# Linear attention before a mixture of experts: q·k in four 64x64 tiles ahead of the state's outputs, the state updated in the turn that made it, k and the rows turned at the turn's end

## The chip, the cores and the metric

The kernel runs on one core of a Trainium2 chip. The metric is the device time of one execution in microseconds (us); lower is better. The kernel before takes 355.63 us (median of three runs, 355.38 to 355.9).

## What is computed

```python
# attention: q, k, v, f_logit are (B=4, H=8, S=768, D=48), float32
f = 1 / (1 + exp(-f_logit))
for t in range(S):
    state = f[:, :, t, :, None] * state + einsum('bhd,bhe->bhde', k[:, :, t], v[:, :, t])
    y[:, :, t] = einsum('bhd,bhde->bhe', q[:, :, t], state)
x = y.transpose(0, 2, 1, 3).reshape(3072, 384)
# mixture of 8 experts: every token goes to the one with the largest logit
e = argmax(x @ w_gate); gate = softmax(x @ w_gate)[e]
out = gate * sigmoid(x @ w_output_gate)[e] * (relu(x @ w1[e]) @ w2[e])
```

## The kernel before

**Two stages.** The attention stage walks over 24 turns t = 0 to 23: four batches b, each of six chunks c = t % 6 of C = 128 steps. The eight heads lie in NP = 4 pairs, a pair on the two halves of the 128 partitions. The expert stage follows: matmuls of line L804 (tokens by w1) and L824 (by w2) with their splits, from about 121 us to the end.

**A chunk.** The decays inside a chunk become running products: `prep(t)` makes f (L209, ScalarE), the products p (`scan_p`, L214, VectorE), their inverses (`scan_i`, L219 and L221, VectorE), and multiplies k and q by them (L225 and L228, GpSimd). What is left is matmuls on TensorE (PE):

- `qk(t)`, L250: k·q of the chunk, per pair two matmuls with 64 rows (a head's half of the partitions) and 128 columns of weights, into two PSUM banks `a_ps`, one for each head of a pair. `mask(t)` copies one bank with ScalarE (L255) and masks it on GpSimd (L256), and masks the other on VectorE (L259); the result is `at`.
- `kn_tr(t)`, L267: k turned, copied by `evac_kn` (L275, ScalarE). No batch's last chunk (c = 5) needs it.
- `out_state(t)`, L310: the state ahead of the chunk by q, in 64x64 tiles, and `out_at(t)`, L318: `at` by v. Both add into y, which lies in two PSUM banks, `two` and the upper half of `one`. The first chunk (c = 0) has no state.
- `state(t)`, L283: turned k by v into the lower half of bank `one`. `state_upd(t)` adds it to the old state and decays it (L297 and L298, VectorE).
- `evac_y(t)`, L332: ScalarE copies y, half a bank at a time, into `xt`; `x_tr(t)`, L338: TensorE turns `xt` into token rows and makes the gate's logits; `evac_x(t)`, L345 and L346: ScalarE copies logits into `lgp` and the rows into `xn`.

**Routing.** After every four turns (two near the end) `route` puts eight small steps into a list: seven VectorE operations (L393 on `lgp`, L396, L397, L398, L400, L401, L391) and one that lets `slots` be made. `fill` takes steps off this list, one or a few at a place. `slots` issues its matmuls at the end of a turn (L424 and L426) into columns of bank `two`, and VectorE reads them (L432, L434). After that, GpSimd sends token rows away with indirect DMAs (L355). The first steps stand in turns 6, 10, 14, 18 and 20, the rank matmuls at the end of turns 7, 11, 15, 19 and 21.

**What sets the order.** Every engine runs its instructions in the order in which the program issues them, and the order of a turn is written out by hand in the loop over t. For each engine of a turn it is, before: TensorE `qk(t)`, `kn_tr(t)`, `x_tr(t-2)`, `out_state(t-1)`, `out_at(t-1)`, `state(t-1)`, ranks; VectorE `state_upd(t-2)`, `scan_p(t+2)`, half of `mask(t)`, `scan_i(t+2)`, with fills between. Loads of later batches are issued on SP's queue at the end of turns (`load`, L183 for v and L190 for q, k and f).

Of the kernel before, what the change touches and what calls it, by code (L numbers as in the profile page):

```python
# [21 lines left out]
C = 128  # L22
NCH = S // C
NP = H // 2
# [8 lines left out]
T_END = 20  # L33
# [24 lines left out]
def warm_up(nc, k, ps, n):  # L58
    for _ in range(n):
        nc.tensor.matmul(ps, k.warm[:, 0:128], k.warm, start=True, stop=True)  # L60
# [72 lines left out]
def attention(ctx, tc, nc, k, kpool, rt, q01, k01, f01, q23, k23, f23, v, wg, xs_dram, r, ex):  # L133
# [14 lines left out]
    q_t = [pl.tile([128, NP, S], F32, name=f"q_t{i}") for i, pl in enumerate((pe, pers))]  # L148
    k_t = [pl.tile([128, NP, S], F32, name=f"k_t{i}") for i, pl in enumerate((pe, pers))]
# [13 lines left out]
    one = psB.tile([128, 512], F32, name="one_ps")  # L163
# [71 lines left out]
    at, aps, kn, xt, xps, yps = {}, {}, {}, {}, {}, {}  # L235
    scomp = {}

    def hot(t):
        return 0 <= t < len(order)

    def qk(t):

        b, c = order[t]
        sl = slice(c * C, (c + 1) * C)
        at[t] = wk.tile([128, 2, NP, C], F32, name="at")
        aps[t] = [psA.tile([128, NP, C], F32, name="a_ps", bufs=2) for par in range(2)]
        for g in range(NP):
            for par in range(2):
                r = slice(64 * par, 64 * par + 64)
                nc.tensor.matmul(aps[t][par][:, g, :], k_t[b % 2][r, g, sl], q_t[b % 2][r, g, sl],  # L250
                                 start=(g == 0), stop=(g == NP - 1))

    def mask(t, par):
        if t == 0 or par:
            nc.scalar.activation(out=at[t][:, par], in_=aps[t][par], func=AF.Copy)  # L255
            nc.gpsimd.affine_select(out=at[t][:, par], in_=at[t][:, par], pattern=[[0, NP], [1, C]],  # L256
                                    compare_op=ALU.is_ge, fill=0.0, base=0, channel_multiplier=-1)
            return
        nc.vector.tensor_tensor(out=at[t][:, par], in0=aps[t][par], in1=k.mask, op=ALU.mult)  # L259

    def kn_tr(t):
        b, c = order[t]
        if c == NCH - 1:
            return
        kps = psA.tile([128, NP, 128], F32, name="kn_ps")
        for g in range(NP):
            nc.tensor.transpose(out=kps[:, g, :], in_=k_t[b % 2][:, g, c * C:(c + 1) * C], identity=k.ident)  # L267
        kn[t] = kps

    def evac_kn(t):  # L270
        if t not in kn:
            return
        kps = kn[t]
        kn[t] = wk.tile([128, NP * 128], F32, name="kn")
        nc.scalar.copy(out=kn[t], in_=kps.rearrange("p g t -> p (g t)"))  # L275

    def state(t):
        b, c = order[t]
        if c == NCH - 1:
            return  # L280
        for h in range(H):
            g, r0 = h // 2, 64 * (h % 2)
            nc.tensor.matmul(s_ps[r0:r0 + 64, g, 0:D], kn[t][:, 64 * h:64 * h + 64],  # L283
                             v_t[b][:, c, 64 * h:64 * h + D],
                             start=(h < 2), stop=(h >= 6), skip_group_check=True)

    def state_upd(t):
        b, c = order[t]
        if c == NCH - 1:
            return  # L290
        end = r.pend[:, t * NP:t * NP + NP].unsqueeze(2).broadcast_to([128, NP, D])
        scomp[t] = states[t % 2]
        new, kv = scomp[t][:, :, 0:D], s_ps[:, :, 0:D]
        if c == 0:
            nc.vector.tensor_tensor(out=new, in0=kv, in1=end, op=ALU.mult)
        else:
            nc.vector.tensor_tensor(out=stmp, in0=kv, in1=scomp[t - 1][:, :, 0:D], op=ALU.add)  # L297
            nc.vector.tensor_tensor(out=new, in0=stmp, in1=end, op=ALU.mult)  # L298
# [23 lines left out]
    def out_y(t):  # L322

        y_at(t)
        out_state(t)
        out_at(t)

    def evac_y(t, halves=(1, 0)):
        if t not in xt:
            xt[t] = wk.tile([128, NP, C], F32, name="xt")  # L330
        for i in halves:
            nc.scalar.copy(out=xt[t][:, i::2, :], in_=yps[t][i])  # L332

    def x_tr(t):

        xps[t] = psB.tile([128, 512], F32, name="x_ps")[:, 0:NP * XW].rearrange("p (g e) -> p g e", e=XW)
        for g in range(NP):
            nc.tensor.matmul(xps[t][:, g, :], xt[t][:, g, :], turn[:, g, :], start=(g == 0), stop=(g == NP - 1))  # L338

    def evac_x(t):  # L340
        if t % 4 == 0:
            xn[t // 4] = xnp.tile([128, 4, RW], F32, name="xn")
            nc.gpsimd.iota(out=xn[t // 4][:, :, DM], pattern=[[C, 4]], base=t * C, channel_multiplier=1,
                           allow_small_or_imprecise_dtypes=True)
        nc.scalar.copy(out=lgp[:, t % 8, :].rearrange("p (g e) -> p g e", e=2 * E), in_=xps[t][:, :, 2 * D:XW])  # L345
        nc.scalar.copy(out=xn[t // 4][:, t % 4, 0:DM].rearrange("p (g e) -> p g e", e=2 * D),  # L346
                       in_=xps[t][:, :, 0:2 * D])
# [18 lines left out]
    def fill(n=1):  # L366
        for _ in range(min(n, len(dq))):
            dq.pop(0)()

    def drain():  # L370
        while dq:
            dq.pop(0)()

    def run_pq(n=None):
        n = len(pq) if n is None else n
        todo, pq[:] = pq[:n], pq[n:]
        for f in todo:
            f()
# [88 lines left out]
    last = len(order) - 1  # L467
# [11 lines left out]
    def pre(t, *names):  # L479
        if hot(t):  # L480
            for nm in names:
                if nm not in done[t]:
                    done[t].add(nm)
                    pre_of[t][nm]()
# [20 lines left out]
    ends, t0 = {}, 0  # L505
# [3 lines left out]
    for t in range(last + 1):  # L509
        ready = len(pq)  # L510
        more = 1 if t < T_END else 0

        fill(more)
        if hot(t - 2):
            evac_y(t - 2, (1,))
        if t not in (0, 2):
            pre(t + 2, "f")
        if hot(t - 2):
            evac_y(t - 2, (0,))
            state_upd(t - 2)  # L520
        if t == 2:
            pre(4, "f")
        pre(t + 1, "mul_k")
        if t + 1 == last:
            done_sb.close()
            ex.open_early()
        fill(more)
        if t > 1:
            pre(t + 2, "scan_p")
        qk(t)  # L530
        mask(t, 1)
        mask(t, 0)
        if t == 0:
            pre(2, "s", "f")
        pre(t + 2, "scan_p", "scan_i")
        if t == 0:
            pre(2, "mul_k")
        fill(more)
        kn_tr(t)
        if t == 0:  # L540
            warm_up(nc, k, one, 4)
        if hot(t - 2):
            x_tr(t - 2)
        evac_kn(t)
        pre(t + 2, "mul_q", "ends")
        if hot(t - 2):
            evac_x(t - 2)
        if t == last:
            ex.split(1, 0, 1, nc.gpsimd)
            route(*ends[t - 2])  # L550
            drain()
        fill(more)
        if T_END <= t < last:
            fill(8)
        pre(t + 3, "s")
        if t == last:
            done_ps.close()
            ex.open_early_psum()
        if hot(t - 1):
            out_y(t - 1)  # L560
        if hot(t - 1):
            state(t - 1)
        if t == last:
            hand_over()
            break
        run_pq(ready)
        if t >= T_END:
            pre(t + 2, "mul_k")
        if t >= T_SCAT:
            scatter(1 if t < T_END else 2)  # L570

        b, c = divmod(t - 3, NCH)
        if t >= 3 and b + 2 < B and c in (0, 2, 4):
            load(b + 2, [("fkq", c, c + 2)])
            if c == 4:
                load(b + 2, [("v", i, i + 2) for i in range(0, NCH, 2)])
        fill(2 if more else 10)
        fill(2 * more)
        if t - 2 in ends:
            route(*ends[t - 2])  # L580
        if t >= T_END:
            scatter(2)
            if len(ex.apart) == T_TOP:
                ex.tokens_in(0, 0, EARLY // TS)
                ex.load_rest(0)
        if t + 1 == last:
            drain()
            assert ex.xq
            ex.split(1, 0, 0, nc.gpsimd)
# [592 lines left out]
```

## Time and profile before

| what | value |
|---|---|
| median of three runs | 355.63 us (355.38 to 355.9) |
| profiled execution | 355.4 us, span of its profile 353.5 us |
| attention, turns 3 to 22 | 22.31 to 112.94 us of the span |
| last turn and hand-over | 112.94 to 121.45 us |
| expert stage | 121.45 us to the end |
| TensorE busy, share of the span | 339.4 us, 96% |
| VectorE, ScalarE, GpSimd busy | 252.1, 202.6 and 213.6 us |
[...]

The span is what the profile shows from the first instruction to the last; 1.9 us of the profiled time lie around it. A busy share over the whole span is an average of two stages; the stage in which something changes has to be looked at by itself. A TensorE record is one pass of a matmul: a float32 matmul of this stage leaves two (16 of L250 in a turn for eight matmuls).

### The profile page before, as it was taken

What the parts mean: (1) busy time and instruction counts of PE and PEld (TensorE: products, weight loads), DVE (VectorE), ACT (ScalarE), POOL (GpSimd) and SP (SyncE); (2) the same over time, 40 slices, a digit from 0 to 9 for tenths busy, and PEclk for the clock granted to TensorE, in tenths of its full rate; (3) what the DMA queues carried; (4) which work ended last, traced back from release to release, by engine and by line L of the source; (5) the groups of instructions that cost most, each with busy time, mean ns of one, the idle gap of its engine ahead of it and who ended that gap; (6) DMA issues with size and microseconds to landing.
All of it is one profiled execution on the core that took longest, in us unless ns stands there. A gap on an engine that the chain in (4) does not pass through costs nothing.

```text
span 353.5 us, 8664 instructions
## 1 busy us (share of the span) xinstructions
PE 339.4 (96%) x3037; PEld 317.5 (90%) x3037; DVE 252.1 (71%) x514; ACT 202.6 (57%) x508; POOL 213.6 (60%) x252
## 2 busy tenths in 40 slices
PE   8889999999999899998999999999999999999992
PEld 2678988898899799997999999999999999999991
DVE  6998989898998676568866766666776766665700
ACT  3576776776775571544853672673673673675510
POOL 8586789899998861000476375276276276187521
PEclk9999999999999999999999999999999999999998
DMA  7999999999408935989659368459468367420101
GB/s 252 350 359 357 346 281 283 307 279 281 158 32 273 270 119 138 190 269 184 194 171 189 115 189 182 136 173 205 111 198 190 116 193 189 135 81 28 60 26 43
DMA packets 75205, 67.64 MB, mean 191 GB/s; under 512 B 30813, under 2 KB 69481, under 8 KB 75152
## 3 DMA queue, kind: packets, MB, share of 16 engines
q1 hardware_dynamic: 70576, 57.34, 59.0%
q0 software_dynamic: 4576, 9.66, 8.1%
q8 instruction: 26, 0.43, 0.5%
q14 instruction: 27, 0.22, 0.2%
HBM read 54.04 MB, written 13.46 MB: 191 GB/s over the span
## 4 chain that ended last, share of the span: by engine, by line
PE 77%; DVE 8%; issue 4%; ACT 3%; DMA 3%; SPq 2%; POOL 1%; POOLq 0%; DVEq 0%; ACTq 0%
PE h_ps L804 27%; PE y_ps L824 20%; PE x_ps L338 6%; PE a_ps L250 5%; PE y_ps L838 5%; PE two_ps L318 3%; PE two_ps L310 3%; PE one_ps L318 3%; PE kn_ps L267 3%; PE one_ps L283 2%; DVE p L214 1%; DVE i L221 1%; SPq L709 1%; DMA xm<-xs_dram 1%; DMA f_t<-in_f 1%
## 5 line engine op out<-in xcount | busy, mean ns | idle before, releaser
L857 POOL DMA_INDIRECT out<-yr,dst x83 | 90.8, 1094 | 59.7 <-ACT yr L856 35.5
L804 PE MATMUL h_ps<-xh,w1h 128*128 128x400 f32 (+6 forms) x192 | 65.3, 340 | 1.1 <-DVE hl L809 1.1
L804 PE MATMUL h_ps<-xh,w1l 128*128 128x400 f32 (+6 forms) x192 | 65.2, 340 | 0.0
L804 PE MATMUL h_ps<-xl,w1h 128*128 128x400 f32 (+6 forms) x192 | 65.2, 340 | 0.0
L809 DVE SCALAR_TENSOR_TENSOR hl<-h_ps,hh 128x256 fp32r<-128x256 f32 (+6 forms) x72 | 39.1, 544 | 32.2 <-ACT hh L808 31.8
L808 ACT ACTIVATE hh<-h_ps 128x256 fp32r<-128x256 f32 (+6 forms) x72 | 34.8, 483 | 42.2 <-PE h_ps L804 40.7
L824 PE MATMUL y_ps<-hh,w2h 128*128 128x256 f32 (+4 forms) x168 | 56.0, 333 | 0.0
L824 PE MATMUL y_ps<-hl,w2h 128*128 128x256 f32 (+4 forms) x168 | 55.9, 333 | 0.0
L824 PE MATMUL y_ps<-hh,w2l 128*128 128x256 f32 (+4 forms) x168 | 55.9, 333 | 0.0
L668 DVE TENSOR_TENSOR w1l<-w1r,w1h 128x768 fp32r<-128x768 f32 x29 | 27.8, 958 | 15.5 <-ACT w1h L667 15.3
L804 PEld LDWEIGHTS h_ps<-xh,w1h 128*128 128x128 f32 x192 | 36.1, 188 | 2.1 <-DVE hl L809 1.5
L804 PEld LDWEIGHTS h_ps<-xl,w1h 128*128 128x128 f32 x192 | 36.1, 188 | 0.6
L804 PEld LDWEIGHTS h_ps<-xh,w1l 128*128 128x128 f32 x192 | 36.1, 188 | 0.6
L228 POOL TENSOR_TENSOR q_t<-q_t,p 128x512 f32<-128x512 f32 x24 | 30.6, 1273 | 4.6 <-DVE p L214 4.5
L824 PEld LDWEIGHTS y_ps<-hh,w2l 128*128 128x128 f32 x168 | 31.7, 188 | 0.6
L824 PEld LDWEIGHTS y_ps<-hl,w2h 128*128 128x128 f32 x168 | 31.6, 188 | 0.7
L824 PEld LDWEIGHTS y_ps<-hh,w2h 128*128 128x128 f32 x168 | 31.7, 188 | 0.6
L214 DVE TENSOR_TENSOR_SCAN p<-f_ps,start_p 128x511 f32<-128x511 f32 x22 | 28.0, 1274 | 3.7 <-ACT start_p L202 2.0
L668 DVE TENSOR_TENSOR w2l<-w2r,w2h 128x768 fp32r<-128x768 f32 x31 | 29.6, 955 | 1.3 <-ACT w2h L667 0.6
L771 ACT CAST xh<-xr 128x400 fp32r<-128x400 f32 (+6 forms) x24 | 12.2, 517 | 32.0 <-DVE xr L765 32.0
L250 PE MATMUL a_ps<-q_t,k_t 64*128 64x128 f32 x384 | 28.3, 285 | 2.1 <-DVE k_t L225 1.2
L355 POOL DMA_INDIRECT xs_dram<-xn,slot x24 | 24.7, 1029 | 7.8 <-issue 3.8
(165 smaller groups left out, 746.4 us busy)
## 6 DMA issues: line engine op xcount, KB each, us to landing
w1r<-in_w SPq DMA_DIRECT2D x32, 384.0 KB, 5.0
w2r<-in_w SPq DMA_DIRECT2D x32, 384.0 KB, 3.0
v_t<-in_v SPq DMA_DIRECT2D x12, 512.0 KB, 9.1
xs_dram<-empty SPq DMA_DIRECT2D x8, 401.0 KB, 10.8
f_t<-in_f SPq DMA_DIRECT2D x6, 512.0 KB, 9.6
q_t<-in_q SPq DMA_DIRECT2D x6, 512.0 KB
k_t<-in_k SPq DMA_DIRECT2D x6, 512.0 KB, 9.6
f_t<-in_f SPq DMA_DIRECT2D x12, 192.0 KB, 6.7
```

Of the source, the lines that this page charges most:

```text
L214: nc.vector.tensor_tensor_scan(out=flat(d["p"])[:, 1:n], data0=flat(d["f"])[:, 0:n - 1], data1=sp[:, 1:n], initial=sp[:, 0:1], op0=ALU.mul ...
L228: nc.gpsimd.tensor_tensor(out=q_t[i][:, :, sl], in0=q_t[i][:, :, sl], in1=d["p"], op=ALU.mult)
L250: nc.tensor.matmul(aps[t][par][:, g, :], k_t[b % 2][r, g, sl], q_t[b % 2][r, g, sl], start=(g == 0), stop=(g == NP - 1))
L318: nc.tensor.matmul(yps[t][g % 2][r0:r0 + 64, g // 2, :], v_t[b][:, c, 64 * h:64 * h + 64], at[t][:, h % 2, g, :], start=((first or c == 0) ...
L338: nc.tensor.matmul(xps[t][:, g, :], xt[t][:, g, :], turn[:, g, :], start=(g == 0), stop=(g == NP - 1))
L355: i = nc.gpsimd.indirect_dma_start(out=xs_dram, out_offset=bass.IndirectOffsetOnAxis(ap=r.slot[:, t:t + 1], axis=0), in_=xn[t // 4][:, t % ...
L668: (eng or self.nc.vector).tensor_tensor(out=to(lo), in0=of(t), in1=to(hi.bitcast(F32)), op=ALU.subtract)
L804: nc.tensor.matmul(ps[:, 0:n], a[:, c, cs], b, start=(i == 0), stop=(i == 3 * KC - 1))
L808: nc.scalar.activation(out=hi, in_=ps[:, 0:n], func=AF.Relu)
L809: nc.vector.scalar_tensor_tensor(out=lo, in0=ps[:, 0:n], scalar=0.0, in1=hi.bitcast(F32), op0=ALU.max, op1=ALU.subtract)
L824: self.nc.tensor.matmul(self.ys[d][:, c0:c0 + n], a, b, start=(f == 0 and i == 0 and part == 0), stop=(f == KF - 1 and i == 2), skip_group ...
L857: self.other_rows(self.nc.gpsimd.indirect_dma_start(out=self.out.rearrange("n (q w) -> (n q) w", q=NQ), out_offset=bass.IndirectOffsetOnAx ...
```

## The change

`qk` makes each product with 64 instead of 128 columns of weights: 16 matmuls in four 64x64 tiles (two row halves by two column halves) instead of eight in two 64x128 tiles. In the turn's order, `out_state`, `out_at` and `state` of t-1 move up to stand directly behind `qk(t)`, and `kn_tr(t)` and `x_tr(t-2)` come after them. `evac_y(t-1)` and `state_upd(t-1)` are issued in the same turn, where they stood in the next. The logits and rows (`evac_x`) are copied at the turn's end, after `prep`'s small steps. VectorE masks ahead of `scan_p`.

```diff
         for g in range(NP):
-            for par in range(2):
-                r = slice(64 * par, 64 * par + 64)
-                nc.tensor.matmul(aps[t][par][:, g, :], k_t[b % 2][r, g, sl], q_t[b % 2][r, g, sl],
-                                 start=(g == 0), stop=(g == NP - 1))
+            for half in range(2):
+                s0, to = c * C + 64 * half, slice(64 * half, 64 * half + 64)
+                for par in range(2):
+                    r = slice(64 * par, 64 * par + 64)
+                    nc.tensor.matmul(aps[t][par][to, g, :], k_t[b % 2][r, g, s0:s0 + 64], q_t[b % 2][r, g, sl],
+                                     start=(g == 0), stop=(g == NP - 1), skip_group_check=True)
...
         fill(more)
-        if hot(t - 2):
-            evac_y(t - 2, (1,))
-        if t not in (0, 2):
+        if t > 0:
             pre(t + 2, "f")
-        if hot(t - 2):
-            evac_y(t - 2, (0,))
-            state_upd(t - 2)
...
-        if t > 1:
-            pre(t + 2, "scan_p")
         qk(t)
+        mask(t, 0)
         mask(t, 1)
-        mask(t, 0)
...
-        pre(t + 2, "scan_p", "scan_i")
-        fill(more)
-        kn_tr(t)
-        if hot(t - 2):
-            x_tr(t - 2)
-        evac_kn(t)
-        pre(t + 2, "mul_q", "ends")
-        if hot(t - 2):
-            evac_x(t - 2)
+        pre(t + 2, "scan_p")
...
         if hot(t - 1):
             out_y(t - 1)
-        if hot(t - 1):
             state(t - 1)
+            if t < last:
+                evac_y(t - 1, (0,))
+                state_upd(t - 1)
+                evac_y(t - 1, (1,))
+        pre(t + 2, "scan_i")
+        fill(more)
+        if t < last:
+            kn_tr(t)
+            if hot(t - 2):
+                x_tr(t - 2)
+            evac_kn(t)
+        pre(t + 2, "mul_q", "ends")
+        pre(t + 3, "s")
+        if hot(t - 2) and t < last:
+            evac_x(t - 2)
+        fill(more)
```

How an ordinary turn stands on TensorE, before (turn 14, c = 2; names as above, with the columns of one matmul's output and how many in a row):

```order
L250 MATMUL a_ps<-q_t_98,k_t_100 128x128 x8
L267 MATMUL kn_ps<-ident,k_t_100 128x128 x4
L338 MATMUL x_ps<-turn,xt 128x112 x4
L310 MATMUL two_ps<-q_t_98,state_106 64x128 x2
L310 MATMUL one_ps<-q_t_98,state_106 64x128 x2
L310 MATMUL two_ps<-q_t_98,state_106 64x128 x2
L310 MATMUL one_ps<-q_t_98,state_106 64x128 x2
L318 MATMUL two_ps<-at,v_t 64x128 x2
L318 MATMUL one_ps<-at,v_t 64x128 x2
L318 MATMUL two_ps<-at,v_t 64x128 x2
L318 MATMUL one_ps<-at,v_t 64x128 x2
L283 MATMUL one_ps<-v_t,kn 64x48 x8
```

And the same turn after the change, where lines are two higher:

```order
L252 MATMUL a_ps<-q_t_98,k_t_100 64x128 x16
L312 MATMUL two_ps<-q_t_98,state_106 64x128 x2
L312 MATMUL one_ps<-q_t_98,state_106 64x128 x2
L312 MATMUL two_ps<-q_t_98,state_106 64x128 x2
L312 MATMUL one_ps<-q_t_98,state_106 64x128 x2
L320 MATMUL two_ps<-at,v_t 64x128 x2
L320 MATMUL one_ps<-at,v_t 64x128 x2
L320 MATMUL two_ps<-at,v_t 64x128 x2
L320 MATMUL one_ps<-at,v_t 64x128 x2
L285 MATMUL one_ps<-v_t,kn 64x48 x8
L269 MATMUL kn_ps<-ident,k_t_100 128x128 x4
L340 MATMUL x_ps<-turn,xt 128x112 x4
```

The products stand in twice as many matmuls, `out_state` (L312) follows them, and the turned k (L269) and rows (L340) have moved from the second and third place to the end.

VectorE of turn 10, in which the steps of a route begin, before; the row of L297 is the state's update of t-2, L259 the mask:

```order
L393 TENSOR_REDUCE xn<-lgp 128x4x16
L297 TENSOR_TENSOR misc<-one_ps,state_107 128x192
L298 TENSOR_TENSOR state_106<-misc,pend 128x4x48
L396 TENSOR_REDUCE misc<-xn 128x4
L214 SCALAR_TENSOR_TENSOR p<-f_ps,start_p_183 128x511
L259 TENSOR_TENSOR at<-a_ps,mask 128x512
L219 RECIPROCAL start_i_187<-p 128x4
L221 SCALAR_TENSOR_TENSOR i<-f_ps,start_i_187 128x512
L397 TENSOR_TENSOR misc<-xn,misc 128x32
L398 SCALAR_TENSOR_TENSOR misc<-misc,first 128x32
L400 TENSOR_REDUCE first<-misc 128x4
L401 TENSOR_TENSOR ohb<-misc,first 128x32
```

And after, from the first route step of that turn on (L395):

```order
L395 TENSOR_REDUCE xn<-lgp 128x4x16
L398 TENSOR_REDUCE misc<-xn 128x4
L261 TENSOR_TENSOR at<-a_ps,mask 128x512
L214 SCALAR_TENSOR_TENSOR p<-f_ps,start_p_183 128x511
L299 TENSOR_TENSOR misc<-one_ps,state_106 128x192
L300 TENSOR_TENSOR state_107<-misc,pend 128x4x48
L219 RECIPROCAL start_i_187<-p 128x4
L221 SCALAR_TENSOR_TENSOR i<-f_ps,start_i_187 128x512
L399 TENSOR_TENSOR misc<-xn,misc 128x32
L400 SCALAR_TENSOR_TENSOR misc<-misc,first 128x32
L402 TENSOR_REDUCE first<-misc 128x4
L403 TENSOR_TENSOR ohb<-misc,first 128x32
```

The first two route steps have come together ahead of the mask, the mask is ahead of L214, and the state's update (L299 and L300) has moved behind both, to the `state` of the same turn.

## Rows read from the trace of the kernel before

**Rows 1.** The page's head: the span, and busy time of each engine with its share and instructions.

```profile
span 353.5 us, 8664 instructions
...
PE 339.4 (96%) x3037; PEld 317.5 (90%) x3037; DVE 252.1 (71%) x514; ACT 202.6 (57%) x508; POOL 213.6 (60%) x252
```

**Rows 2.** Busy time by stretches: turns 3 to 22, and the expert stage. Columns: stretch, its length, busy time (and records) of PE, weight loads, DVE, ACT and POOL, granted clock, DMA share, GB/s.

```profile
22.31:112.94 90.63, 89.81 (x1440) 80.32 (x1436) 81.87 (x167) 63.98 (x193) 78.46 (x81) 1.00 0.91 266
121.45:353.40 231.95, 223.96 (x1313) 219.06 (x1309) 145.93 (x298) 122.49 (x269) 110.79 (x114) 0.99 0.55 149
```

**Rows 3.** The same view of six single turns: 3, 13 (c = 1), 14 (ordinary), 15 (ordinary, with ranks), 17 (c = 5) and 18 (c = 0).

```profile
22.31:27.49 5.18, 4.90 (x81) 4.20 (x77) 4.84 (x7) 3.35 (x11) 3.84 (x6) 1.00 1.08 358
67.81:71.84 4.03, 4.03 (x62) 3.75 (x60) 3.09 (x5) 3.34 (x10) 3.83 (x5) 1.00 1.09 292
71.84:76.47 4.63, 4.63 (x80) 4.18 (x76) 4.56 (x10) 3.34 (x10) 4.43 (x5) 1.00 1.10 280
76.47:81.32 4.85, 4.85 (x86) 4.37 (x82) 4.32 (x9) 3.27 (x11) 4.66 (x6) 1.00 1.11 275
85.95:90.44 4.49, 4.31 (x77) 3.79 (x73) 3.90 (x7) 2.76 (x9) 4.29 (x5) 1.00 1.01 338
90.44:94.62 4.18, 4.18 (x65) 3.61 (x61) 3.93 (x8) 3.24 (x10) 3.98 (x5) 1.00 0.31 112
```

**Rows 4.** TensorE in order of time, the ordinary turn 14. Columns: start, length (us), line, output and inputs, tile and shape, records merged.

```profile
71.84 1.16 PE L250 MATMUL a_ps<-q_t,k_t 64*128 64x128 f32 x16
72.93 0.66 PE L267 MATMUL kn_ps<-ident,k_t 128*128 128x128 f32 x4
73.43 1.04 PE L338 MATMUL x_ps<-turn,xt 128*128 128x112 f32 x8
74.40 0.33 PE L310 MATMUL two_ps<-q_t,state 64*64 64x128 f32 x2
74.41 0.33 PE L310 MATMUL one_ps<-q_t,state 64*64 64x128 f32 x2
...
74.56 0.28 PE L310 MATMUL two_ps<-q_t,state 64*64 64x128 f32 x2
...
74.78 0.28 PE L310 MATMUL two_ps<-q_t,state 64*64 64x128 f32 x2
...
75.00 0.44 PE L318 MATMUL two_ps<-at,v_t 128*64 128x128 f32 x4
...
75.92 0.62 PE L283 MATMUL one_ps<-v_t,kn 128*64 128x48 f32 x16
```

**Rows 5.** VectorE in order of time, turns 10 and 11 and the read of the ranks in turn 12; the same columns, some instructions left out.

```profile
53.98 0.56 DVE L393 TENSOR_REDUCE xn<-lgp 128x64 f32<-128x256 f32 x1
...
55.61 0.20 DVE L396 TENSOR_REDUCE misc<-xn 128x4 f32<-128x32 f32 x1
55.71 1.27 DVE L214 TENSOR_TENSOR_SCAN p<-f_ps,start_p 128x511 f32<-128x511 f32 x1
...
57.69 1.22 DVE L221 TENSOR_TENSOR_SCAN i<-f_ps,start_i 128x512 f32<-128x512 f32 x1
58.83 0.18 DVE L397 TENSOR_TENSOR misc<-xn,misc 128x32 f32<-128x32 f32 x1
...
59.86 0.36 DVE L297 TENSOR_TENSOR misc<-one_ps,state 128x192 f32<-128x192 f32 x1
...
60.53 1.27 DVE L214 TENSOR_TENSOR_SCAN p<-f_ps,start_p 128x511 f32<-128x511 f32 x1
61.72 0.67 DVE L259 TENSOR_TENSOR at<-a_ps,mask 128x512 f32<-128x512 f32 x1
...
62.50 1.22 DVE L221 TENSOR_TENSOR_SCAN i<-f_ps,start_i 128x512 f32<-128x512 f32 x1
...
63.80 0.19 DVE L432 TENSOR_TENSOR rk<-two_ps,ohb 128x32 f32<-128x32 f32 x1
```

**Rows 6.** ScalarE in order of time, the second half of turn 10.

```profile
56.08 0.58 ACT L275 COPY kn<-kn_ps 128x512 f32<-128x512 f32 x1
57.02 0.20 ACT L231 COPY pend<-p 128x4 f32<-128x4 f32 x1 [0.35 <-DVE p L214]
57.12 0.20 ACT L345 COPY lgp<-x_ps 128x64 f32<-128x64 f32 x1
57.22 0.48 ACT L346 COPY xn<-x_ps 128x384 f32<-128x384 f32 x1
57.59 0.22 ACT L202 ACTIVATE start_p<-f_t 128x4 f32<-128x4 f32 x1
57.90 0.19 ACT L204 COPY p<-start_p 128x1 f32<-128x1 f32 x1
```

**Rows 7.** Waits between 22 and 113 us: who waited for whom, us in total, times, longest. These are two of them.

```profile
ACT xt L332 <- PE one_ps L283: 13.3, 16, 1.1
...
PEld x_ps L338 <- ACT xt L332: 1.6, 4, 0.5
```

**Rows 8.** SP's queue around 61 us, first the order of the loads, then the time from issue to landing of the one v load issued between 60.8 and 61.5 us, and of all three issued between 58 and 72 us.

```profile
60.59 1.78 SPq L183 DMA_DIRECT2D v_t<-in_v  x3
...
DMA to landing us min/median/max: 8.4/8.4/8.4
DMA to landing us min/median/max: 8.4/9.1/9.8
```

More of the change, by code (lines that the diff above doesn't have):

```diff
@@ L513, in attention @@
         fill(more)
-        if hot(t - 2):
-            evac_y(t - 2, (1,))
-        if t not in (0, 2):
+        if t > 0:
             pre(t + 2, "f")
-        if hot(t - 2):
-            evac_y(t - 2, (0,))
-            state_upd(t - 2)
-        if t == 2:
-            pre(4, "f")
         pre(t + 1, "mul_k")
@@ L527, in attention @@
         fill(more)
-        if t > 1:
-            pre(t + 2, "scan_p")
         qk(t)
+        mask(t, 0)
         mask(t, 1)
-        mask(t, 0)
         if t == 0:
             pre(2, "s", "f")
-        pre(t + 2, "scan_p", "scan_i")
-        if t == 0:
-            pre(2, "mul_k")
-        fill(more)
-        kn_tr(t)
-        if t == 0:
-            warm_up(nc, k, one, 4)
-        if hot(t - 2):
+        pre(t + 2, "scan_p")
+        if t == last:
             x_tr(t - 2)
-        evac_kn(t)
-        pre(t + 2, "mul_q", "ends")
-        if hot(t - 2):
             evac_x(t - 2)
-        if t == last:
             ex.split(1, 0, 1, nc.gpsimd)
@@ L551, in attention @@
             drain()
[L552 to L556, printed above, removed]
             done_ps.close()
@@ L560, in attention @@
             out_y(t - 1)
-        if hot(t - 1):
             state(t - 1)
+            if t < last:
[3 more added lines that the diff above has]
+        pre(t + 2, "scan_i")
+        if t == 0:
+            pre(2, "mul_k")
+        fill(more)
+        if t < last:
+            kn_tr(t)
+            if t == 0:
+                warm_up(nc, k, one, 4)
+            if hot(t - 2):
[6 more added lines that the diff above has]
+        fill(more)
+        if T_END <= t < last:
+            fill(8)
         if t == last:
```

## The prediction

> **What bounds the kernel now.** I read the page's head first: TensorE is busy for 96% of the span [rows 1]. As this is a mean over two stages, the view by stretches comes next. From turn 3 to turn 22 TensorE is busy for 89.81 of 90.63 us at full clock; VectorE has 81.87 there, GpSimd 78.46, ScalarE 63.98 [rows 2]. So TensorE sets the pace of attention, but VectorE has only 9 us less work. The expert stage, which the change doesn't touch, is bound by TensorE too (223.96 of 231.95 us [rows 2]): what attention gains or loses ahead of 121.45 us is passed on to the end.
>
> The stretches of single turns show what a turn costs: 4.63 us for an ordinary one, 4.03 without `out_state` (c = 1), 4.18 without `state` (c = 0), 4.49 without the turned k (c = 5), .22 more where ranks are computed (4.85), and 5.18 in turn 3 [rows 3]. In all but turns 3 and 17 TensorE is busy for the whole turn, so a turn is the sum of its blocks. The timeline of turn 14 gives these: qk 1.09 (71.84 to 72.93), turned k .50, rows .97, `out_state` .60, `out_at` .92, `state` .55 (75.92 to 76.47, the end of the stretch) [rows 3, 4].
>
> **What TensorE saves.** In `out_state`, four 64x64 tiles run side by side and each such group takes .11 us (74.56 to 74.78 are two), but the first group takes .16 and the last .22 (74.78 to 75.00) [rows 4]. The first and the last stand where the form of the tiles changes, and I read the .05 and .11 over as the price of a change of form. qk has eight pairs of records now: eight times .11 is .88, and the remaining .21 of its 1.09 is such a price at both ends.
>
> After the change qk has 32 records, four tiles each: eight groups of .11, as many as now. The column split itself is therefore worth nothing. But `out_state` follows in the same form, so qk keeps only the price ahead of it: .88 + .05 = about .92 (a saving of .17), and `out_state` loses its slow first group: .60 - .06 = .54. The other four blocks keep their lengths. An ordinary turn becomes .92 + .54 + .92 + .55 + .50 + .97 = 4.39 with rounding, .24 less. A turn with c = 0 likewise falls from 4.18 to 3.94. With c = 1 there is no `out_state`, and qk keeps the price at its end: 4.03 to 3.95. With c = 5, 4.39 less the .50 of the turned k, and about .1 since the rows now bear a change of form: 4.00; the .18 that TensorE waits there [rows 3] for the copy of y (L338 on L332, 1.6 us in four waits [rows 7]) goes, because the rows are now turned a whole turn after that copy. Ranks cost .12 instead of .22, because they now follow matmuls of their own form.
>
> Turns 3 to 22 are 11 ordinary ones (turn 3 among them), three each with c = 0, 1 and 5, and five of these have ranks: 11 x 4.39 + 3 x 3.94 + 3 x 3.95 + 3 x 4.00 + 5 x .12 = 84.6 us against 90.63, a saving of **6.07 us**. Turn 3's .55 over an ordinary turn may be kept in part, as it falls in the time of the first loads; I give back half, **.28**. Turns 0 to 2, where loads set the pace, and turn 23 with the hand-over I leave at nothing; both ends for these are -.5 and +.5, about one turn's saving each way.
>
> **What comes back: the ranks.** The rank matmuls write bank `two`, VectorE reads them with L432, and the next turn's first `out_state` (or `out_at`) writes the same bank. Now qk, turned k and rows, 1.09 + .50 + .97 = 2.56 us [rows 4], stand between the ranks and `out_state`: L432 starts at 63.80 in turn 12 [rows 5], and there is no wait. After, only qk's .92 is left, and L432 is later on VectorE, because the route steps start later: L393 needs the logits and rows that ScalarE copies, and these copies now stand last in the turn.
>
> When L393 can start: turned k ends .92 + .54 + .92 + .55 + .50 = 3.43 into the turn, and ScalarE gets it some .1 later. Then, by the steps of [rows 6], k's copy about .5 (its record is .58), `pend` .10, the start of p .31, p about as long, logits .10, rows .48: 5.3 us, that is **1.0 us** (.9 to 1.0) into the next turn of 4.39.
>
> From there VectorE has a row of work without a gap: L393 .56 and L396 .10; a turn's own work, which is update .67 (59.86 to 60.53), `scan_p` 1.19, mask and reciprocal .78 (61.72 to 62.50), `scan_i` 1.14 (57.69 to 58.83), together 3.78; the five other steps 1.03 (58.83 to 59.86); again 3.78; and L432 .19 [rows 5]. That is 9.44 us. TensorE reaches `out_state` after two turns and one qk. The wait is the difference:
>
> - turns 10 and 11: 1.0 + 9.44 - (4.39 + 4.12 + .92) = 1.01
> - turns 14 and 15: the same less (4.39 + 4.51 + .92) = .62
> - turns 6 and 7: the update falls out in the first and is one operation in the second, so about 1.0 less work, against 3.94 + 4.07 + .92: .53
> - turns 18 and 19: as 6 and 7, with one more read of the bank (.2): .73
> - turns 20 and 21: the steps all stand at the end of turn 20, on half the tokens (L393 about .4): 1.0 + .4 + .10 + 1.03 + 3.78 + .19 = 6.5, against 4.39 + .12 + .92: 1.07
>
> Together **3.96 us**. Each tenth in the 1.0 moves this by half a us.
>
> **What comes back: a load.** The three v loads of batch 2 are issued from 60.59 us on. The second takes 8.4 us to land (about 69.5), the third 9.8 [rows 8]. Loads on this queue come in order, so the first lands about one load's time (some 2 us: the third, issued about 1 us after the second, lands 2.3 after it) ahead of the second: 67.5, at the latest 69.5. `out_at(12)` in turn 13 needs it, at 67.81 + 1.09 + .50 + .97 = 70.37 now; after, turns 3 to 12 save 3.2 us by the lengths above and lose 1.5 to the first two waits, and its new place, behind qk alone, is 1.5 earlier in the turn: about 67.1. I take **.45 us**; bounds 0 and 2.
>
> **What costs nothing.** The state's update now waits for `state` inside the same turn, at 2.93 us; VectorE gets there after mask and `scan_p`, about 2.8 us, so it waits some tenths, out of a slack of 4.39 - 3.78 = .6. ScalarE's copies of y no longer stand ahead of the next turn's mask, where they waited 13.3 us for `state` [rows 7]; they still wait, but nobody is late by it. GpSimd's 78.46 us fit into 84.6 + 4.4. If VectorE's .6 is used up, each tenth is lost in every turn, 2 us in all; that is in the rivals below.
>
> **Sum.** -6.07 + .28 + 3.96 + .45 = -1.4 us, against the profiled execution's 355.4 (span 353.5 and 1.9 around it): 354.0. The median of the runs shown is 355.63, .2 higher, so **354.3 us** for the median. With L393 at .8 to 1.3 into the turn it is 353.3 to 355.8.
>
> **Rivals.**
>
> *The waits on VectorE are smaller* (chance .2). VectorE's operations overlap, and a wait in one turn gives it time in the next. With L393 half a us earlier the waits come to 1.5 and the time to 351.8; without any, 350.3. Against it: a VectorE that is busy for 81.87 us can't leave much slack in 84.6.
>
> *VectorE becomes the bound* (.2). If its work (81.87 us busy) and the new waits for `state` come to more than 89 us in these turns, what TensorE saves is lost again: .2 us of it per turn more than I count is 4 us, 358; .1 gives 356. It decides from the point where mask, `scan_p`, update and `scan_i` with their waits take over 4.4 us in an ordinary turn. For it speaks that the update moves behind `scan_p`, so that `scan_i` waits with it; against it the .6 us of slack.
>
> *Four tiles run two by two* (.1), the case on the other side. If the tiles of the same row half didn't load and run side by side, qk's 32 records would be 16 groups of .11: 1.8 instead of .92, .9 more in each of 24 turns, 21 us, of which the waits of 4 us above and the 6 us of savings are to be taken away: about **+13, 369**. Against it: in `out_state` the records into `one` start at 74.41, 10 ns behind those into `two` at 74.40, and use the same row halves [rows 4]. [...] The order of tiles in qk is another than in `out_state` (two row halves of one column half first), and no row shows that order, so the chance is not nil. If the number of instructions were the limit (80 and 76 records of matmuls and weight loads in an ordinary turn now [rows 3], 32 more after), the result would be on this side as well; but 74.40 to 76.47 holds 48 matmuls and as many loads at 22 ns each, and the new turn needs one in 23 ns on the mean.
>
> **How the numbers follow.** The forecast's own case has .5, with 353.3 to 355.8. The two rivals about VectorE bring the range to 351.5 and 357.5; left out are the four tiles and the low end without any wait, 2 in 10 in all. .2% (.7 us) is about what a measurement of this kernel can tell from no change. Faster than 354.9: .35 of the .5 and the first rival, .55. Slower than 356.3: .13 of the second rival and the four tiles, .23. Between: .22.
>
> **What would show it.** Right: an ordinary turn of 4.39 us from qk to qk, with eight groups of .11 in qk; `out_state` right behind it without a slow first group; five waits of TensorE for L434 (L432 now), .5 to 1.1 us each, at the start of turns 8, 12, 16, 20 and 22; one wait in turn 13 for the v load; the expert stage starting about 1.4 us earlier and as long as before. Wrong: qk longer than 1.1 us; waits of `out_at` for the mask or of `out_state` for the update in ordinary turns; turns of 4.6 without waits, which would say that the price of a change of form isn't saved where two blocks share one.

## The result

The changed kernel takes 359.2 us (median of 14 runs, 356.99 to 365.88) against 355.89 us of the kernel before on the same chips (14 runs): the ratio is 1.0100, with a 95% interval of 1.0076 to 1.0124. It is slower by 1%, 3.3 us by the medians, where 354.3 was forecast with a range up to 357.5. Eight of the 14 runs lie at 357.0 to 359.3 us and five at 361.7 to 362.2; the traced one is of the first group, so what the second loses besides is open.

The profiled execution took 359.14 us. The head of its page, which answers to [rows 1]; PE is TensorE:

```profile
span 357.4 us, 9436 instructions
...
PE 337.8 (95%) x3420; PEld 316.2 (88%) x3421; DVE 253.1 (71%) x514; ACT 200.0 (56%) x508; POOL 213.4 (60%) x252
```

TensorE has 383 more matmul records and 384 more weight loads, and is busy for 1.6 us less. The stretches that answer to [rows 2] and to an ordinary turn of [rows 3], turn 4 here:

```profile
22.31:116.77 94.46, 88.47 (x1757) 79.38 (x1756) 82.41 (x163) 61.61 (x195) 78.61 (x81) 1.00 0.91 254
125.23:357.40 232.17, 224.01 (x1313) 219.11 (x1309) 146.37 (x299) 122.81 (x271) 110.68 (x114) 0.99 0.56 149
26.72:31.13 4.41, 4.41 (x93) 4.08 (x92) 3.95 (x7) 3.22 (x12) 3.28 (x4) 1.00 1.09 353
```

The expert stage lasts as long as before (232.2 against 231.95 us). Turns 3 to 22 take 94.46 instead of 90.63 us: nearly all of the loss is there (3.8 us of 3.9 by the spans). Yet an ordinary turn that isn't held up lasts 4.41 us, as forecast. TensorE sat idle for 6 us of the 94.46, where it had sat idle for .8 of 90.63.

Where it sat idle, in order of time (TensorE's matmuls; in brackets the idle time before the row and what ended it):

```profile
48.04 0.49 PE L285 MATMUL one_ps<-v_t,kn 128*64 128x48 f32 x9 [0.95 <-issue]
...
56.29 0.76 PE L252 MATMUL a_ps<-q_t,k_t 64*64 64x128 f32 x18 [1.30 <-issue]
...
63.20 0.43 PE L312 MATMUL one_ps<-q_t,state 64*64 64x128 f32 x2 [1.18 <-issue]
...
85.27 0.33 PE L312 MATMUL two_ps<-q_t,state 64*64 64x128 f32 x2 [0.63 <-DVE rk L434]
...
96.25 0.32 PE L320 MATMUL two_ps<-at,v_t 128*64 128x128 f32 x1 [0.57 <-issue]
...
113.23 0.33 PE L312 MATMUL two_ps<-q_t,state 64*64 64x128 f32 x2 [0.96 <-DVE rk L434]
```

Two of the long ones are the forecast waits for the ranks' read. The other four stand in the middle of a row of like matmuls, and nothing that the profile shows ended them: "issue". They are not at random places. Between them TensorE works off the same number of records each time (the stretches from one to the next; the x behind PE and PEld count matmuls and weight loads):

```profile
40.70:48.02 7.33, 6.39 (x126) 5.64 (x126) 6.42 (x14) 4.68 (x13) 5.49 (x5) 1.00 1.07 278
48.02:56.28 8.26, 6.95 (x125) 6.21 (x125) 6.69 (x12) 5.39 (x18) 7.85 (x9) 1.00 1.11 259
56.28:63.20 6.91, 5.72 (x126) 5.15 (x126) 5.72 (x13) 3.74 (x11) 4.99 (x7) 1.00 1.12 252
89.78:96.25 6.47, 5.91 (x125) 5.16 (x125) 5.64 (x10) 3.77 (x11) 6.07 (x7) 1.00 0.75 266
```

That is 250 to 252 each, and with the few records that this view leaves out 256: counted from the start of the trace, TensorE stops at records 1216, 1472, 1728, 1984, 3008 and 3264, steps of 256 or multiples of it (a first stop, of .3 us, is at record 960). I call 256 records between two such places a block. What goes with them is seen in the DMA queue q8, named "instruction". What the queues moved between 53.3 and 55.1 us, and what from there to 56.2, shortly before TensorE went on at 56.29 (columns: packets, MB, share of 16 engines):

```profile
q1 hardware_dynamic: 328, 0.31, 91.4%
q8 instruction: 1, 0.02, 5.1%
...
q1 hardware_dynamic: 230, 0.22, 92.3%
```

One instruction packet of 16 KB landed by 55.1 us (at 54.95), and TensorE goes on 1.3 us after it. At the other long stops it is the same: packets end 1.3 to 1.5 us ahead of 48.03, 63.20 and 96.25. The number of packets fits the steps too. From 40.70 to 96.25 us, 2048 records of TensorE, q8 brought 8 packets, one for 256 records. Over the whole span it brought 29 (0.48 MB) against 26 (0.43 MB) in the kernel before, three more for 767 more matmuls and weight loads, 3.0 times 256, while the other instruction queue, q14, brought 27 in both. So I read the stops as TensorE having run out of instructions.

An ordinary turn of the kernel before uses 256 records up in 7.6 us (80 and 76 in 4.63 us [rows 3]), one of the changed kernel in 6.1 us (185 in 4.41). Between two stops with a stop in each, a block took 6.5 to 8.3 us. With the loads running (DMA share 1.07 to 1.12 in the first three stretches above) a block thus took longer than the 6.1 us in which the faster TensorE uses one up. But it isn't a fixed rate. Three blocks between 63.20 and 82.46 us passed without a stop, at the same DMA share; two of them:

```profile
70.48:76.24 5.76, 5.76 (x128) 5.19 (x128) 4.28 (x7) 4.43 (x16) 5.56 (x6) 1.00 1.09 288
76.24:82.46 6.22, 6.22 (x129) 5.83 (x127) 5.98 (x15) 3.93 (x12) 5.84 (x8) 1.00 1.09 293
```

What differs is when the packet starts. In each of the seven blocks that end with a stop, the packet that I take for the next block's started 3.9 to 5.5 us after TensorE had entered the block (for the three stops from 48 to 63 us: 40.70 to 45.47, 48.03 to 53.49, 56.29 to 60.51); in these three it was 2.7 to 3.1 us. With 1.0 to 1.5 us for the packet and the 1.3 to 1.5 behind it, I estimate that the next block can be run some 5 us after TensorE has entered this one in the good case and 8 in the bad. Why the packet starts later at one time than at another isn't shown. From 98 us on the DMA share is low (.36 up to 116 us) and no stop is left.

### The profile page after: what moved, and what is told of

The parts are those of the page before. It is cut to its first block, busy times and chain, and to the rows that moved or that the text cites. A ratio compares the mean times of both kernels' runs of the same rounds, so it can differ in the third digit from the quotient of the medians.

```text
span 357.4 us, 9436 instructions
## 1 busy us (share of the span) xinstructions
PE 337.8 (95%) x3420; PEld 316.2 (88%) x3421; DVE 253.1 (71%) x514; ACT 200.0 (56%) x508; POOL 213.4 (60%) x252
## 4 chain that ended last, share of the span: by engine, by line
PE 66%; DVE 13%; DMA 7%; issue 6%; SPq 3%; POOL 3%; ACT 2%; POOLq 0%; DVEq 0%; ACTq 0%
PE h_ps L803 25%; PE y_ps L823 19%; PE y_ps L837 5%; PE a_ps L252 4%; PE x_ps L340 3%; DVE p L214 3%; PE two_ps L320 2%; DVE i L221 2%; DMA xs_dram<-xn,slot 2%; PE kn_ps L269 2%; DMA w1r<-in_w 2%; PE one_ps L320 2%; PE one_ps L285 2%; PE two_ps L312 1%; SPq L708 1%
## 5 line engine op out<-in xcount | busy, mean ns | idle before, releaser
L803 PEld LDWEIGHTS h_ps<-xh,w1h 128*128 128x128 f32 x192 | 36.1, 188 | 1.9 <-DVE hl L808 1.3
L803 PEld LDWEIGHTS h_ps<-xh,w1l 128*128 128x128 f32 x192 | 36.1, 188 | 0.6
L803 PEld LDWEIGHTS h_ps<-xl,w1h 128*128 128x128 f32 x192 | 36.1, 188 | 0.6
L252 PE MATMUL a_ps<-q_t,k_t 64*64 64x128 f32 x768 | 28.3, 276 | 4.1 <-issue 1.6
L214 DVE TENSOR_TENSOR_SCAN p<-f_ps,start_p 128x511 f32<-128x511 f32 x22 | 28.0, 1273 | 2.4 <-ACT start_p L202 2.2
```

What stands on the lines that cost most here:

```text
L214: nc.vector.tensor_tensor_scan(out=flat(d["p"])[:, 1:n], data0=flat(d["f"])[:, 0:n - 1], data1=sp[:, 1:n], initial=sp[:, 0:1], op0=ALU.mul ...
L252: nc.tensor.matmul(aps[t][par][to, g, :], k_t[b % 2][r, g, s0:s0 + 64], q_t[b % 2][r, g, sl], start=(g == 0), stop=(g == NP - 1), skip_gro ...
L803: nc.tensor.matmul(ps[:, 0:n], a[:, c, cs], b, start=(i == 0), stop=(i == 3 * KC - 1))
```

## The experiments

The question was how the loss divides between the four tiles and the new order. Except for one group, of which the text says so, the kernel before took 355.75 to 356.02 us on the chips used.

**The two halves apart.** The new order with qk as it was:

```diff
-            for half in range(2):
...
+            for par in range(2):
+                r = slice(64 * par, 64 * par + 64)
+                nc.tensor.matmul(aps[t][par][:, g, :], k_t[b % 2][r, g, sl], q_t[b % 2][r, g, sl],
+                                 start=(g == 0), stop=(g == NP - 1))
```

> The changed order of the turn, with qk in two 64x128 tiles as before (16 records a turn). Theory A (TensorE ran out of instructions: in the changed kernel it stops at record 1216 of its matmuls and weight loads and then at multiples of 256 behind it, each time some 1.4 us after a 16 KB packet of its instruction queue has landed, and four tiles need 32 records more of matmuls and loads each turn): no stop at a multiple of 256; an ordinary turn of about 4.62 us, the c = 5 turns .25 and ranks .1 shorter than before, waits of TensorE for the ranks' read (L434 less the two lines) together about 1.4 us; time 354.5 to 356, within 1 us of the kernel before. Rival B (the order itself is what costs: VectorE's update behind scan_p and the copies at the turn's end): 358 to 360, as the changed kernel.

Measured: 358.07 us, 1.0061 of the kernel before (1.0017 to 1.0105): in rival B's range, not in theory A's. And the other half, the order of the kernel before with the changed `qk` alone:

```diff
-            for par in range(2):
-                r = slice(64 * par, 64 * par + 64)
+            for half in range(2):
+                s0, to = c * C + 64 * half, slice(64 * half, 64 * half + 64)
+                for par in range(2):
...
```

> qk in four 64x64 tiles, in the order of the kernel before. Theory A: TensorE's work is as long as before (4.63 us an ordinary turn when it does not stop), but 256 instructions last 6.3 instead of 7.6 us there and a fetch took 5.3 to 8.3 us in the changed kernel, so there are stops at multiples of 256 of together 3 to 6 us before 97 us, and the time is 358 to 362. Rival B: as before, 355 to 356.5.

Measured: 359.37 us, 1.0092 (1.0044 to 1.0140), in theory A's range. Each half costs by itself, and the two don't add up: by the ratios 2.2 and 3.3 us apart, 3.6 together. In e1 the long waits of TensorE's matmuls and weight loads up to 125 us are these (who waits for whom, us in total, times, longest; two at 120 us, which the kernel before has as well, are left out), and up to 100 us no matmul's wait is put down to "issue":

```profile
PEld two_ps L310 <- DVE rk L432: 3.2, 4, 1.5
...
PE two_ps L318 <- DMA v_t<-in_v: 1.0, 1, 1.0
```

In e2 the weight loads wait thus, with TensorE's records at 1728, 2752 and 3008 when it goes on:

```profile
55.11 0.46 PEld L252 LDWEIGHTS a_ps<-q_t,k_t 64*64 64x64 f32 x16 [0.66 <-issue]
...
81.92 0.10 PEld L426 LDWEIGHTS <-upper 128*128 128x128 bf16 x1 [0.74 <-issue]
88.36 0.19 PEld L252 LDWEIGHTS a_ps<-q_t,k_t 64*64 64x64 f32 x3 [0.66 <-issue]
```

So the stops go with the tiles and the ranks' waits with the order, which is what theory A said. The sizes were less good: e2's traced execution (356.77) was its fastest of four and shows 2 us of stops, less than the 3 to 6 expected; e1 was expected 2 us faster than it came out. Its ranks' read cost 3.2 us instead of 1.4 and the v load 1; whether that is all, or the order costs besides, as rival B says, is left to the runs below.

**The ranks in another bank.** The ranks were put into the free columns of the bank of x:

```diff
-        ps = rank_ps[:, col:col + n * E].rearrange("p (n e) -> p n e", e=E)
+        ps = xroom[0][:, col:col + n * E].rearrange("p (n e) -> p n e", e=E)
...
+        xroom[0] = xb[:, NP * XW:NP * XW + 40]
```

> The changed kernel, with the ranks in the 40 free columns of bank x_ps instead of bank two, so that out_state does not wait for their read. Theory A: the waits for L434 at five turns (about 2.5 us in the changed kernel) are gone, but an earlier TensorE meets its instruction packets earlier, so part comes back as stops: 356.5 to 358.5. Rival C (the ranks' waits are what made the changed kernel slower): 355 or less.

> The changed order with qk in two 64x128 tiles and the ranks in bank x_ps. Theory A: neither stops nor waits for the ranks; what is left is the shorter c = 5 turns (.25 each), cheaper ranks (.1 each) and turn 3 (.5): 353.5 to 354.8, faster than the kernel before. Rival B: 357 or more.

Measured: 366.51 us (1.0279) with four tiles and 365.66 (1.0283) with two. This place was badly chosen. The ranks now have to wait until ScalarE has copied the rows out of the same bank, at the end of a turn (e4; first matmul of the ranks):

```profile
45.77 0.18 PE L427 MATMUL x_ps<-ohb,upper 128*128 128x32 bf16 x1 [1.83 <-ACT xn L348]
```

1.1 to 1.8 us five times in e4, and .8 to 2.0 in e3, is worse than what was taken away. Neither run says anything on the theories, but for one thing: with four tiles there are again stops at records 960, 1216, 1984 and 3008, and with two tiles there are none.

**The ranks earlier.** The ranks' matmuls and their read were moved up in the turn, behind the state's update and ahead of `scan_i`:

```diff
+        if t < last:
+            run_pq(ready)
         pre(t + 2, "scan_i")
...
-        run_pq(ready)
```

Three kernels with this idea and one with useless work (its diff is below) ran first on another chip, on which the kernel before took 402.2 us (381.01 to 404.96) at a granted clock of .95.

> The changed order with qk in two 64x128 tiles (e1), and the ranks made and read right behind the state's update instead of at the turn's end, so that out_state of the next turn finds bank two free. e1 waited about 3.4 us for the ranks' read (L432) and 1.2 us for the v load in turn 13, and its expert stage began at 123.5 us. Theory A (in the order alone it is the ranks' read and the load that cost): L432 waits under .8 us together, the load's wait 1 to 2 us, the expert stage begins at 120 to 121.5 us, time 354 to 355.8, no stop at a multiple of 256. Rival B (VectorE's order costs in every turn, the ranks only show it): expert stage at 123 us or later, 357 or more.

> The changed kernel, with the ranks made and read right behind the state's update. Theory A (instruction supply): the waits for L434 (2.5 us in the changed kernel) fall under .8 us, but TensorE still stops at multiples of 256, together 5 us or more, as nothing has fewer instructions: 356.5 to 359.5 and not faster than f1. Rival C (only the ranks' read cost): 353 to 355.

> The changed kernel with one useless matmul of 512 columns ahead of the turned k (into the same bank, overwritten) in each of 18 turns from turn 3 on: some .21 to .3 us of TensorE's time each with two instructions, 4 to 5 us in all, of which the waits for the ranks may hide 1.5. Theory A (instruction supply): 256 instructions last longer (about 6.3 instead of 6.0 us), so the stops at multiples of 256 shrink from 6 us to 2 to 4 and most of the added time is hidden: 358 to 361 against 359.2. Rival D (the stops don't depend on how fast TensorE uses instructions up): 362 to 364.

> The changed order, ranks early, the first v piece of a batch loaded ahead of the last pieces of f, k and q, qk in two 64x128 tiles up to turn 17 and in four 64x64 tiles from turn 18, where the loads of the attention stage are over. Theory A: no stop at a multiple of 256 of more than .3 us, turns 18 to 22 of 4.4 us, no wait for the v load; 1 us ahead of f1: 352.8 to 354.5. Rival: four tiles stop TensorE in turns 18 to 22 as well, 355 or more.

Measured: 401.99, 407.77, 407.15 and 402.75 us. No time of these can be held against the expectations. In their traces the ranks' waits of f1 are gone up to turn 19 and turn 13 waits 3.5 us for v; f2 and f3 (four tiles) stop at multiples of 256, f1 and f4 don't.

**The cleanest pair.** f1 and f2 again, both with the first v piece loaded ahead of the last pieces of f, k and q, so that neither the ranks nor v are in the way:

```diff
+            if c == 2:
+                load(b + 2, [("v", 0, 2)])
             if c == 4:
-                load(b + 2, [("v", i, i + 2) for i in range(0, NCH, 2)])
+                load(b + 2, [("v", i, i + 2) for i in range(2, NCH, 2)])
```

> The changed order with qk in two 64x128 tiles, the ranks made and read right behind the state's update, and the first v piece of a batch loaded ahead of the last pieces of f, k and q (in f1 turn 13 waited 3.5 us for it, on a chip whose kernel before took 402 us). Theory A: no stop at a multiple of 256, waits for the ranks' read under .8 us together, for v under .5; the expert stage begins at 119.5 to 121 us, time 353.5 to 355.5. Rival B (the order costs in every turn): 357 or more.

> g1 with qk in four 64x64 tiles in every turn: the changed kernel without its waits for ranks and v. Theory A (instruction supply): stops at multiples of 256 of 4 to 7 us before 100 us, which is what TensorE would save: 355.5 to 360, slower than g1 by 1 us or more. Rival C (with ranks and v out of the way the four tiles gain their .2 us a turn): 350 to 353, faster than g1.

Measured: two tiles 357.15 us, 1.0037 (1.0020 to 1.0055); four tiles 362.88 us, 1.0189 (1.0104 to 1.0275). g1 missed theory A's range: with ranks and v out of the way the order still costs 1.3 us, and where it does is looked at below. g4 is slower than expected too. But the two kernels differ in `qk` alone, and the four tiles cost 5.7 us, not gain. In the two traces, first g1 from turn 3 to turn 19, busy in every one of its 74.91 us, and then the places where g4 sat idle for instructions:

```profile
22.65:97.56 74.91, 74.91 (x1206) 67.35 (x1206) 69.28 (x129) 51.71 (x167) 65.42 (x69) 1.00 1.06 290
```

```profile
47.71 0.44 PE L285 MATMUL one_ps<-v_t,kn 128*64 128x48 f32 x9 [0.92 <-issue]
55.41 0.76 PE L252 MATMUL a_ps<-q_t,k_t 64*64 64x128 f32 x18 [0.80 <-issue]
62.59 0.38 PE L312 MATMUL one_ps<-q_t,state 64*64 64x128 f32 x2 [1.46 <-issue]
75.83 0.44 PE L320 MATMUL one_ps<-at,v_t 128*64 128x128 f32 x4 [0.42 <-issue]
82.93 0.49 PE L269 MATMUL kn_ps<-ident,k_t 128*128 128x128 f32 x3 [0.98 <-issue]
90.85 0.54 PE L252 MATMUL a_ps<-q_t,k_t 64*64 64x128 f32 x9 [1.33 <-issue]
97.82 0.44 PE L320 MATMUL one_ps<-at,v_t 128*64 128x128 f32 x4 [1.17 <-issue]
```

These are seven stops of 7.1 us (an eighth, at 40.58, is .4), again 256 records apart or twice that. All of the loss falls there: g4 begins turn 20 at 103.78 us, 6.2 behind g1, and loses nothing to it from there to the expert stage. And they are longer than in the changed kernel, which waits for the ranks besides. Record 3264 runs at 97.82 us in g4 and at 96.25 in the changed kernel: taking a wait away from TensorE didn't bring it there any earlier, it only made it wait for instructions instead. That is how a bound behaves, though these are two single executions.

**Four tiles where the loads are over.** As g1, with four tiles from turn 18 on:

```diff
+            if t < 18:
+                for par in range(2):
...
+                continue
             for half in range(2):
```

> g1 with four tiles from turn 18 on only (the kernel of f4, again, as f4's chip was slow as a whole). Theory A: like g1 up to turn 17, turns 18 to 22 some .2 us shorter each without stops: .5 to 1 us ahead of g1, 352.8 to 355. Rival: stops at multiples of 256 in turns 18 to 22 as well, slower than g1.

Measured: 357.04 us, 1.0028 (.9992 to 1.0064): the same as g1's 357.15, not .5 to 1 us better. In the traced execution (358.6) the rival came true in part: TensorE stops in turn 19, at record 2753, within one of a multiple of 256 behind the changed kernel's 1216, while loads still run (DMA share 1.09 in turn 18).

```profile
97.01 0.76 PE L258 MATMUL a_ps<-q_t,k_t 64*64 64x128 f32 x17 [1.39 <-issue]
```

Two more such places, at 80.35 and 88.74 us, where qk still has two tiles, hold its weight loads up for .4 each. So with two tiles stops are rare and short, not impossible. Turns 21 and 22 are held by something else (below).

**Slower use of instructions.** One useless matmul a turn in the changed kernel:

```diff
         kps = psA.tile([128, NP, 128], F32, name="kn_ps")
+        if t > 2:
+            warm_up(nc, k, kps.rearrange("p g t -> p (g t)"), 1)
```

> The changed kernel with one useless matmul of 512 columns in each of 18 turns (the kernel of f3, again, for the same reason; there the stops at multiples of 256 came to about 3.5 us). Theory A (instruction supply): most of the 4 to 5 us added is hidden by smaller stops and waits: 358 to 361. Rival D (the stops don't depend on how fast instructions are used up): 362 to 364.

Measured: 364.33 us (359.76 to 366.05), just above the rival's range. In the traced execution, its fastest, the stops at multiples of 256 did shrink from 6 to 4 us, and its expert stage began at 125.0 us against 125.23. The other three executions (363.37 to 366.05) lost all of the added time, and they were not traced. This experiment settles nothing.

**What g1 still loses.** g1 is ahead of the kernel before when turn 20 begins (97.56 against 98.89 us), and 1.1 us behind at the expert stage (122.53 against 121.45). What its TensorE waits for between is VectorE and what follows from it:

```profile
104.10 0.33 PE L310 MATMUL two_ps<-q_t,state 64*64 64x128 f32 x2 [0.68 <-DVE start_i L219]
106.76 0.17 PE L424 MATMUL two_ps<-ohb,upper 128*128 128x16 bf16 x1 [0.52 <-ACT xt L332]
111.09 0.32 PE L318 MATMUL two_ps<-at,v_t 128*64 128x128 f32 x1 [0.65 <-POOL at L256]
```

In turns 20 to 22 the steps of the last routes and of the choice of the first expert stand on VectorE ahead of the mask. These turns take 16.5 us in g1 and 14.05 in the kernel before. (In the changed kernel itself, whose ranks are read later, they take 14.5, as forecast: what follows is about g1's order.) h1 takes the order of the kernel before from turn 18 on:

```diff
-        fill(more)
+        if t < SW:
+            fill(more)
...
+        else:
+            fill(more)
+            if hot(t - 2) and t > SW:
+                evac_y(t - 2, (1,))
...
```

> g1 up to turn 17, and from turn 18 on the order of the kernel before (two tiles throughout). g1 is 1.3 us ahead of the kernel before at the start of turn 20 (97.56 against 98.89 us) and 1.1 behind at the expert stage, with waits for VectorE in turns 20 to 22. If those last turns in the new order are what g1 loses, the expert stage begins at 119.8 to 120.6 us and the time is 353.8 to 355.2, ahead of the kernel before. If the rest of the loss lies elsewhere (the loads shifted, the hand-over), 355.8 to 357.5.

Measured: 355.47 us (11 runs) against 355.75 (15 runs), .9990 (.9979 to 1.0000), 1.7 us faster than g1 did. That lies between the two expected ranges; but as nothing else was changed against g1, the last turns are where g1's order lost what it had gained, and not every turn, as rival B had it. Of its gain of 1.3 us, .3 is left: the traced execution has one stop at a multiple of 256 even with two tiles (.52 us of "issue" at 87.44) and begins the expert stage at 121.15 us. It is the best version found, but its interval reaches 1.0000, so that it is faster than the kernel before isn't shown.

## Why the prediction was wrong

**TensorE's own work: right.** An ordinary turn without a wait is 4.41 us against 4.39, one with c = 0 3.96 against 3.94. In turn 4, `out_state` follows qk without a slow first group, and qk takes .92 us (26.72 to 27.64):

```profile
26.72 1.10 PE L252 MATMUL a_ps<-q_t,k_t 64*64 64x128 f32 x32
27.64 0.27 PE L312 MATMUL two_ps<-q_t,state 64*64 64x128 f32 x1
...
28.19 0.44 PE L320 MATMUL two_ps<-at,v_t 128*64 128x128 f32 x4
```

What I read as the price of a change of form is saved here, where two blocks share a form, and four tiles run side by side in this order too: 32 records in .92 us, .115 for a group of four. The rival "two by two", with 1.8 us for qk, falls. (Its price was mis-added besides: 21 us less 4 and 6 are 11, and if the waits are only not added, about 16; not 13.)

**The ranks' read: right in kind, near in size.** 3.96 us in five waits were forecast; four waits with 2.6 us are there (weight loads of L312 for L434, longest 1.2), and one of the five is missing. In e1, which has no stops for instructions, they come to 3.2, so I put the smaller sum down to VectorE catching up while TensorE stops; that was not tried by itself. The v load: .45 forecast, no wait in the changed kernel, whose turn 13 is late anyway, and 1.0 in e1. In the changed kernel, loads of k, v and f issued on SP's queue at 59.22, 63.89 and 66.58 us landed at 66.57, 72.44 and 76.87, in that order.

**The step that failed** stands at the end of the third rival: "If the number of instructions were the limit". It took the pace of the shortest burst, 22 ns each over 96 records [rows 4], for what TensorE can be fed with, and left the matter there: the sum holds nothing for instructions that come late. A burst of 96 records is less than half of a block. Over the stretch with the stops, 40.70 to 96.25 us, TensorE got one 16 KB packet per 256 records, at a mean DMA share of 1.05. The blocks that end with a stop took 6.3 to 8.3 us, not 256 times 22 ns = 5.6. The DMA share of 1.1 stood in the rows of the turns [rows 3], and the count of records too; what was not done is to put the two together: 256 records in 6.1 us against some 7.6 before. Seven stops with 5.8 us of idle weight loads ("issue", .30, .36, 1.07, 1.55, 1.42, .33 and .81) are missing from the sum. Turns 3 to 22 took 9.9 us more than the forecast lengths of 84.6. The seven turns with a stop (5, 7, 8, 10, 11, 17 and 18) account for 7.2 of it, as they took 36.1 us where the forecast lengths give 28.9; turns 12, 16 and 22, which wait for the ranks, for 2.4.

**VectorE as the bound: not in an ordinary turn.** Its .6 us of slack was enough up to turn 19 (g1 is busy without a gap there). In turns 20 to 22 the prediction costed only the ranks, and in the changed kernel that was right: 14.5 us against its 14.4. With the ranks made earlier it was not: there g1 loses 2.4 us to VectorE.

## What to carry to other kernels

Splitting an instruction into two that run side by side cost no time on the engine here (qk took .92 us with 32 records, 1.09 with 16), but it cost instructions, and these came at one 16 KB packet per 256 records while the loads kept the DMA share at 1.05: count the records per us of a stage that is busy with loads, and compare it with the packets of the instruction queue. Stops put down to "issue" in the middle of a row of like matmuls, a fixed number of records apart (256), are what I read as late instructions here. When a wait is taken out of such a stage and the next one grows by as much, stop looking at waits.

## What was not expected of the hardware

In the changed kernel q8 brought one packet of 16 KB for 256 records of TensorE (8 for 2048 from 40.70 to 96.25 us), and TensorE went on 1.3 to 1.5 us after it had ended, at each stop. With the loads of the attention stage running, a block took 6.5 to 8.3 us from stop to stop, and 5.8 to 7.3 where no stop ended it.

In g1, a product of 128x8 elements on VectorE took 1.71 us; its like in the kernel before (L413) took .17:

```profile
99.21 0.17 DVE L412 TENSOR_TENSOR top<-key,mx 128x8 f32<-128x8 f32 x1
99.41 1.71 DVE L413 TENSOR_TENSOR key<-top,num 128x8 f32<-128x8 f32 x1
101.15 0.16 DVE L414 TENSOR_REDUCE mx<-key 128x1 f32<-128x8 f32 x1
```

```profile
99.77 1.30 POOL L225 TENSOR_TENSOR k_t<-k_t,i 128x512 f32<-128x512 f32 x1
101.00 0.65 POOL L256 TENSOR_SCALAR_AFFINE_SELECT at<-at 128x512 f32<-128x512 f32 x1
```

It ends at 101.12 us as GpSimd's product of k (L225) ends at 101.07, but begins .36 us ahead of it. In the kernel before, VectorE's ran from 99.89 to 100.06 us and GpSimd's product of k from 100.91 on. What lengthened it isn't shown. The same operation took 2.17 us in g4, which also has the ranks made early and the new order to the end, and .17 in the changed kernel, e1 and h1. In g1 VectorE works without a gap from there up to L219, for which TensorE waits until 104.10 us, so the 1.5 us are likely a part of the 2.4 that g1 loses in turns 20 to 22; no run takes them out alone.

In e1's traced execution TensorE waited 2.26 us for VectorE in the expert stage, at 167 us, and the granted clock was .50 for 3.4 us from 168.4 on; in the kernel before the same wait is 1.15 us and the granted clock is 1.00 (165 to 171 us). That execution (360.29 us) is the longest of e1's four, and its expert stage is 3.0 us longer than the kernel before's; the 2.1 us that e1 loses ahead of that stage (which begins at 123.52 against 121.45 us) lie before it.
